# A planner that sets the order of every instruction: a finer rule for the port that VectorE and GpSimd share, lags by producing engine, four passes

## The chip, the cores and the metric

The kernel runs on one core of one Trainium2 chip. The metric is the device time of one execution in microseconds (us); three runs of the kernel before were timed. PE is TensorE, DVE VectorE, ACT ScalarE, POOL GpSimd, SP SyncE, whose queue issues most DMAs.

## The reference

Three layers follow each other on inputs of 8 batches, 8 heads, 576 positions and 64 numbers a head. Weights come as 64-bit floats.

```python
pos_block = np.arange(576) // 64
scores = np.where(pos_block[:, None] >= pos_block[None, :], q @ k.T / 8, -1e9)   # by batch and head
x = softmax(scores) @ v                              # heads side by side: 8 x 576 x 512
gate = sigmoid(sum(conv_w[j] * shift(x, 4 - j) for j in range(5)))   # causal, by channel
x = (gate * (x @ w_val)) @ w_out
xk, xr = (mu * x + (1 - mu) * shift(x, 1) for mu in (mu_k, mu_r))
out = sigmoid(xr @ w_r) * (relu(xk @ w_k) ** 2 @ w_v)               # d_ff 1024
```

## The kernel before

Every fp32 factor is split in two fp16 halves (high and low), and a product takes three matmul parts. Attention runs in 32 steps of two heads (a pair). A pair has nine score tiles (`S`, lines 748 to 763, 288 in all), which lie in turn in two halves of one PSUM tile, `sp`. For each tile: `S` on PE, `max` on DVE (line 774), `nb` (the scaled negative maximum, a 128x1 instruction on POOL or DVE, line 463), `exp` on ACT (line 777), then `rs` (row sums and reciprocal), `phi` (high half of the probabilities, `P`) and `plo` (low half, line 460 on DVE), and a DMA transpose `ptr`. Tile k+2 writes the half of `sp` that the exponential of tile k reads. `pv` (line 822) multiplies with the values into `xps`; `xhi`, `xlo`, `tap`, `conv` (line 953, reads PSUM) and `gate` make the next layers' input `xx` and the gate `tg`.

The other layers run over 13 chunks of 384 or 192 rows, all through `layer` (line 998): `V` (x @ w_val) with `gv`, `ghi`, `glo` behind it (tiles `tmp`, `gg`), `O` (w_out) with `T`, `mix`, `ymax`, `Tr`, `mixr`, `rhi`, `rlo`, then `khi`, `klo`, `Z` (w_r, the factor `wr`), `K` (w_k, tile `w3`) with `t`, `sq`, `k2h`, `k2l` (tile `kx`), and `W` (w_v, the factor `wv`) with `lo` and the store `lout`. A `W` or `Z` step is six matmuls of 512 columns. Before the first chunk the weights are loaded (`w1ld` and the like, line 554), converted in three integer steps on DVE (lines 510 to 516) and split (`h`, `o`), and `w_r`, `w_v` are read twice, first for a bound (`wrm`, `wvm`). `lodq`, `lodk`, `lodv` are the low halves of q, k and v (line 460; tiles `natqk`, `natv`); `bxr` scales `xx` anew at the end of a batch.

What order all this is issued in is not the order of the code. Each piece is an entry of `Plan` with a label (with ' for the pieces of the start), a rank, a cost on each engine that may take it, what it reads and writes, and whether it is one of those that use the port that DVE and POOL share (`share=True`). `Plan.order` walks through a modelled time: the engine that can start earliest takes the ready entry of lowest rank. `Plan.latest` walks back from the end and gives each entry its latest time, which is the rank of the next pass. The tables `OFF`, `OFF2` (added to the ranks), `PATIENCE` (how long a second engine must wait before it may take an entry) and `PREF` (the first engine) have one number per label. The framework keeps the order so found on each engine and adds the waits.

The costs and lags are numbers of the plan alone; on the chip an instruction starts as soon as its engine and its semaphores let it.

Of the kernel before, what the change touches and what calls it, by code (L numbers as in the profile page):

```python
# [32 lines left out]
class Plan:  # L33
# [5 lines left out]
    CROSS, SAME, SWITCH, DMA_OUT, DMA_IN, DMA_SET = 140, 120, 90, 1000, 650, 920  # L39
    BLOCK, WINDOW = 150, 3413  # L40
# [31 lines left out]

    def order(self, off={}, patience={}, pref={}, base=None):
# [40 lines left out]
        for _ in ops:  # L114
            while True:
                best = None
                for e, w in waiting.items():
                    if w:
                        t = max(free[e], min(w.values()))
# [10 lines left out]
            n = min((rank[x] for x, r in waiting[e].items() if r <= t))[1]  # L130
# [3 lines left out]
            if (e == POOL or (e == DVE and ops[n][7])) and ns > 130:  # L134
                t = max(t, port)
# [39 lines left out]
    def latest(self):  # L175
# [1149 lines left out]
```

## Time and profile before

| what | value |
|---|---|
| median of 3 runs | 1270.04 us (1266.98 to 1271.29) |
| the profiled execution, its own time | 1269.61 us |
| its span, first to last instruction | 1267.6 us |
| mean granted TensorE clock | 0.925 |
| busy: PE, DVE, ACT, POOL | 1027.4, 910.5, 729.3, 599.4 us |
| DMA: bytes moved, mean | 140.78 MB, 111 GB/s |

The span is 2 us shorter than the execution's time. A row of the timeline or of the waits names line, engine, operation and output<-inputs; in brackets stands how long the engine was idle before it and what ended that. A busy PE is not one at full speed: its clock is granted in two levels, and a clock of 0.9 in a stretch means that a fifth of it ran at the lower.

### The profile page before, as it was taken

How to read it: one execution, taken by the hardware profiler on the slowest of the kernel's cores; microseconds unless marked ns; L12 is line 12 of the kernel's file. 1: busy time of each engine (PE TensorE's matmuls, PEld its weight loads, DVE VectorE, ACT ScalarE, POOL GpSimd, SP SyncE). 2: the span in 40 equal slices, each digit the busy share in tenths (PEclk: the TensorE clock that was granted, in tenths of full speed). 3: DMA queues.
4: the chain of work that ended last, by engine and by line, in shares of the span. 5: the costliest groups of instructions: out<-in, count | busy, mean ns of one | idle time of the engine just before them, and what ended most of it. 6: DMA issues, size and time to landing. Idle time of an engine off the chain costs nothing. (4 is left out here: it accounts for less than half of the span.)

```text
span 1267.6 us, 20049 instructions
## 1 busy us (share of the span) xinstructions
PE 1027.4 (81%) x6695; PEld 544.5 (43%) x6695; DVE 910.5 (72%) x1984; ACT 729.3 (58%) x1583; POOL 599.4 (47%) x1185
## 2 busy tenths in 40 slices
PE   1244446699779878999899888989998799999997
PEld 0011223355434445545455454544444454444464
DVE  5787887877668787767787687677776787656441
ACT  4565566454556766656566666566666666544331
POOL 2356573322536554544646436347465546352321
PEclk9975567799899998999899889999898899999999
DMA  8597884325455774517547672366556655133000
GB/s 230 139 223 185 198 210 94 62 65 126 89 117 107 148 147 89 100 28 169 101 88 152 130 159 44 74 133 109 117 107 131 131 108 108 37 70 69 10 17 21
DMA packets 416630, 140.78 MB, mean 111 GB/s; under 512 B 402960, under 2 KB 402960, under 8 KB 416528
## 3 DMA queue, kind: packets, MB, share of 16 engines
q1 hardware_dynamic: 416032, 137.94, 51.1%
q0 software_dynamic: 496, 1.58, 0.4%
q8 instruction: 52, 0.85, 0.3%
q14 instruction: 50, 0.41, 0.1%
HBM read 49.31 MB, written 9.44 MB: 46 GB/s over the span
## 5 line engine op out<-in xcount | busy, mean ns | idle before, releaser
L463 POOL TENSOR_SCALAR smalls<-smalls 128x1 f32<-128x1 f32 (+2 forms) x607 | 212.3, 355 | 358.1 <-DVE smalls L774 213.8
L998 PEld LDWEIGHTS <-w 128*128 128x128 f16 x2640 | 246.3, 99 | 157.7 <-issue 28.3
L777 ACT ACTIVATE P<-sp,smalls 128x448 f32<-128x448 f32 (+4 forms) x288 | 183.8, 639 | 170.5 <-DVE smalls L774 45.2
L774 DVE TENSOR_REDUCE smalls<-sp 128x1 f32<-128x448 f32 (+4 forms) x288 | 145.4, 515 | 114.6 <-PE sp L763 68.4
L998 PE MATMUL fp<-wv,kx 128*128 128x512 f16 (+1 forms) x888 | 211.3, 383 | 6.7 <-DVE th L1197 5.4
L998 PE MATMUL fp<-kx,w 128*128 128x384 f16 (+1 forms) x1248 | 200.7, 314 | 2.7 <-DVE tmp L1179 2.7
L998 PEld LDWEIGHTS <-kx 128*128 128x128 f16 (+1 forms) x1332 | 124.3, 99 | 151.7 <-issue 28.2
L758 PE MATMUL sp<-qkT 128*128 128x128 f16 (+5 forms) x288 | 85.8, 313 | 100.5 <-ACT P L777 69.0
L457 POOL TENSOR_TENSOR kx<-tmp,kx 128x384 f16<-128x384 f32 (+1 forms) x144 | 132.0, 920 | 65.8 <-ACT kx L448 38.1
L998 PE MATMUL fp<-gg,w 128*128 128x385 f16 (+1 forms) x624 | 108.4, 328 | 11.2 <-DVE tmp L1100 9.0
L998 PE MATMUL fp<-wr,kx 128*128 128x512 f16 (+1 forms) x444 | 111.2, 391 | 6.2 <-DVE th L1197 4.8
L998 PE MATMUL fp<-xx,w 128*128 128x384 f16 (+1 forms) x768 | 107.6, 296 | 2.5 <-DVE tmp L1179 1.0
L953 DVE SCALAR_TENSOR_TENSOR tg<-xps,smalls,tg 128x575 f32<-128x575 f32 (+3 forms) x128 | 102.7, 803 | 0.3 <-ACT xx L448 0.2
L460 DVE SCALAR_TENSOR_TENSOR P_a<-P,smalls,P_a 128x576 f16<-128x576 f32 (+1 forms) x128 | 92.9, 733 | 3.5 <-ACT P_a L448 3.1
L758 PE MATMUL sp<-qkT,q2T 128*128 128x128 f16 (+5 forms) x288 | 91.4, 317 | 0.0
L822 PE MATMUL xps<-PT,natv 128*64 128x512 f16 (+1 forms) x720 | 76.2, 332 | 17.8 <-DMA xx<-in_moe_w_v_dram 10.9
L448 ACT ACTIVATE P_a<-P,smalls 128x576 f16<-128x576 f32 (+1 forms) x122 | 79.4, 664 | 18.2 <-DVE smalls L237 12.6
L1179 DVE TENSOR_TENSOR tmp<-fp,tmp 128x384 f32<-128x384 f32 (+1 forms) x104 | 54.3, 523 | 42.6 <-ACT tmp L1177 41.6
L1177 ACT ACTIVATE tmp<-fp 128x384 f32<-128x384 f32 (+1 forms) x104 | 48.1, 463 | 55.2 <-PE fp L998 54.8
L758 PEld LDWEIGHTS <-q2T 128*128 128x128 f16 x288 | 27.8, 101 | 113.6 <-issue 107.1
L822 PEld LDWEIGHTS <-natv 128*64 128x64 f16 x768 | 47.5, 122 | 42.5 <-issue 25.1
L450 POOL TENSOR_SCALAR kx<-tmp 128x384 f16<-128x384 f32 (+1 forms) x71 | 41.2, 584 | 48.4 <-DVE tmp L1100 35.5
(177 smaller groups left out, 1724.0 us busy)
## 6 DMA issues: line engine op xcount, KB each, us to landing
rawv<-in_v_dram SPq DMA_DIRECT2D x32, 288.0 KB, 3.4
out_dram<-th SPq DMA_DIRECT2D x35, 256.0 KB, 2.1
rawk<-in_k_dram SPq DMA_DIRECT2D x31, 288.0 KB, 3.2
rawq<-in_q_dram SPq DMA_DIRECT2D x31, 288.0 KB, 3.5
q2T<-qkT SPq DMA_DIRECT2D x60, 144.0 KB, 2.5
xx<-in_moe_w_v_dram SPq DMA_DIRECT2D x8, 512.0 KB, 4.6
tg<-in_moe_w_v_dram SPq DMA_DIRECT2D x7, 512.0 KB, 4.7
tg<-in_moe_w_k_dram SPq DMA_DIRECT2D x4, 512.0 KB, 4.6
```

The lines of the kernel that those rows point to most:

```text
L448: nc.scalar.activation(out=o, in_=i, func=AF.Copy, scale=scale)
L457: eng[e].tensor_tensor(out=o, in0=a, in1=b, op=ALU.subtract)
L460: nc.vector.scalar_tensor_tensor(out=o, in0=a, scalar=scale, in1=b, op0=ALU.mult, op1=ALU.subtract)
L463: eng[e].tensor_scalar(out=o, in0=i, scalar1=a, scalar2=b, op0=op0, op1=op1)
L758: nc.tensor.matmul(sall[:, base + c0:base + c1], qts[e][:, o + 64 * (2 * t - 1):o + 64 * (2 * t + 1)], kt[:, o + c0:o + c1], start=(e == 0 ...
L774: nc.vector.tensor_reduce(out=mx, in_=sp, op=ALU.max, axis=AX.X)
L777: nc.scalar.activation(out=P[:, 0:n], in_=sp, func=AF.Exp, scale=small["posc"][p % 3], bias=nb, accum_out=sm)
L822: nc.tensor.matmul(o, w, x, start=start, stop=stop, skip_group_check=True)
L953: lambda t=t: nc.vector.scalar_tensor_tensor(out=acc[:, t:S], in0=ps[:, 0:S - t], scalar=cx[:, 4 - t:5 - t], in1=acc[:, t:S], op0=ALU.mult ...
L998: nc.tensor.matmul(o, w, y, start=(k == i == j == 0), stop=(k == nk - 1 and i == len(ps) - 1), skip_group_check=True)
L1177: lambda fp=fp, t=t: nc.scalar.activation(out=t, in_=fp, func=AF.Relu, scale=2.0 ** -42))
L1179: lambda fp=fp, t=t: nc.vector.tensor_tensor(out=t, in0=fp, in1=t, op=ALU.mult))
```

## The change

No piece of work is added or removed. In the planner: (1) a POOL entry that is no DMA, and a DVE entry with `share`, wait in the plan until the port is free, but an engine may take another ready entry meanwhile; DVE's shared entries always hold the port, POOL's only from 300 ns on (before: any of either over 130 ns held it, and the engine stood still for it). (2) The lag between two entries goes by the engine that produces: 200, 120, 135, 70 ns for PE, DVE, ACT, POOL; before 140 across engines and 120 on one. (3) Two passes back and forth instead of one, then a last pass with the ranks of `latest`, 160 single corrections (`NUDGE`) and a third table (`OFF3`): four passes of `order`. (4) New numbers in all tables, a cost of 1040 for `pv` instead of 950, and slightly other spacings T0 and T2.

```diff
@@ -36,8 +36,10 @@
 
 
 
-    CROSS, SAME, SWITCH, DMA_OUT, DMA_IN, DMA_SET = 140, 120, 90, 1000, 650, 920
-    BLOCK, WINDOW = 150, 3413
+
+    LAG = {"PE": 200, "DVE": 120, "ACT": 135, "POOL": 70}
+    SWITCH, DMA_OUT, DMA_IN, DMA_SET = 90, 1000, 650, 920
+    BLOCK, WINDOW, SMALL = 150, 3413, 300
 
     def __init__(self):
         self.ops = []
@@ -70,6 +72,12 @@
     def transpose(self, lab, rank, blocks, reads, writes, fn, *args):
         self.add(lab, rank, self.BLOCK * blocks, [SP], reads, writes, fn, *args, dma=2)
 
+    def lag(self, d, e, f):
+
+        if e is None or f is None or e == f == PE:
+            return 0
+        return self.DMA_OUT if self.ops[d][6] else self.LAG[e]
+
     def order(self, off={}, patience={}, pref={}, base=None):
         ops = self.ops
         users = [[] for _ in ops]
@@ -81,6 +89,7 @@
         start = [0.0] * len(ops)
         taken = [None] * len(ops)
         free = {e: 0.0 for e in (PE, DVE, ACT, POOL, SP, None)}
+        turns = {DVE: [o[7] for o in ops], POOL: [not o[6] for o in ops]}
         lane = ring = port = 0.0
         live, warm, last, flying = [], False, True, []
         waiting = {e: {} for e in free}
@@ -92,10 +101,7 @@
             for f, _ in choice:
                 t = 0.0
                 for d in deps:
-                    e = taken[d]
-                    lag = 0 if e is None or (e == PE and f == PE) else (
-                        self.DMA_OUT if ops[d][6] else self.SAME if f == e else self.CROSS)
-                    t = max(t, finish[d] + lag)
+                    t = max(t, finish[d] + self.lag(d, taken[d], f))
                 waiting[f][n] = t if f == first else t + patience.get(lab, 1500.0)
 
         finish = [0.0] * len(ops)
@@ -116,7 +122,11 @@
                 best = None
                 for e, w in waiting.items():
                     if w:
-                        t = max(free[e], min(w.values()))
+                        turn = turns.get(e)
+                        if turn:
+                            t = max(free[e], min(max(r, port) if turn[x] else r for x, r in w.items()))
+                        else:
+                            t = max(free[e], min(w.values()))
                         if best is None or t < best[0]:
                             best = (t, e)
                 if not flying or (best and flying[0][0] > best[0]):
@@ -127,12 +137,12 @@
                     free[SP] = max(free[SP], lane - 950)
                 done(n)
             t, e = best
-            n = min((rank[x] for x, r in waiting[e].items() if r <= t))[1]
+            turn = turns.get(e)
+            n = min((rank[x] for x, r in waiting[e].items() if r <= t and not (turn and port > t and turn[x])))[1]
             for f, _ in ops[n][2]:
                 del waiting[f][n]
             ns = dict(ops[n][2])[e]
-            if (e == POOL or (e == DVE and ops[n][7])) and ns > 130:
-                t = max(t, port)
+            if turn and turn[n] and (e == DVE or ns >= self.SMALL):
                 port = t + ns
                 self.busy["port"] += ns
             start[n], taken[n] = t, e
@@ -188,18 +198,10 @@
         back = [0.0] * len(ops)
 
         def ready(n):
-            e = where[n]
             t = self.DMA_OUT if ops[n][6] else 0
             for u in users[n]:
-                f = where[u]
-                if e is None or f is None:
-                    lag = 0
-                elif ops[n][6]:
-                    lag = self.DMA_OUT
-                else:
-                    lag = 0 if e == f == PE else self.SAME if e == f else self.CROSS
-                t = max(t, back[u] + lag + (self.DMA_SET if ops[u][6] else 0))
-            waiting[e][n] = t
+                t = max(t, back[u] + self.lag(n, where[n], where[u]) + (self.DMA_SET if ops[u][6] else 0))
+            waiting[where[n]][n] = t
 
         for n in range(len(ops)):
             if not left[n]:
@@ -223,10 +225,17 @@
         return [end - x for x in back]
 
     def plan(self):
-        best = self.order(OFF, PATIENCE, PREF)
+        self.order(OFF, PATIENCE, PREF)
         for _ in range(ITER):
-            best = self.order(OFF2, PATIENCE, PREF, self.latest())
-        return best
+            self.order(OFF2, PATIENCE, PREF, self.latest())
+        base = self.latest()
+        seen = {}
+        for n, o in enumerate(self.ops):
+            seen.setdefault(o[0], []).append(n)
+        for lab, a, b, ns in NUDGE:
+            for n in seen[lab][a:b]:
+                base[n] += ns
+        return self.order(OFF3, PATIENCE, PREF, base)
 
     def issue(self):
         for n in self.plan():
@@ -237,105 +246,182 @@
                 fn(*args)
-ITER = 1
+ITER = 2
...
-    'K': 4.3, "K'": 7.2, "KX'": -203.8, 'O': -8.3, "O'": 36.8, 'S': -0.5, "S'": -3.9, 'T': -5.4,
+    'K': 4.3, "K'": 7.2, "KX'": -203.8, 'O': -7.0, "O'": 42.3, 'S': -0.5, "S'": -3.9, 'T': -5.4,
...
-            add("pv", e + 0.1 * part, 950, [PE], [("PT", second(p), t) for t in range(NT + 1)] + ["natvh", "natvl", ("dv", 0), ("dv", 1)],
+            add("pv", e + 0.1 * part, 1040, [PE], [("PT", second(p), t) for t in range(NT + 1)] + ["natvh", "natvl", ("dv", 0), ("dv", 1)],
...
-T0, T1, T2 = 19.8, 26.8, 71.3
+T0, T1, T2 = 20.4, 26.8, 71.2
```

Three places in the built programs show what moves. In the changed file every line behind the tables stands 86 lines lower, and 9 lines lower in the first functions.

PE, score tiles 244 and 245 of 288 (counted from 0; lines 758 and 763, both heads' factors `qkT` and `q2T`), before. The first two rows are the end of tile 244, the last two the begin of a `Z` step (`wr`):

```order
L763 LDWEIGHTS q2T_93
L763 MATMUL sp<-qkT_91,q2T_93 64x64
L758 LDWEIGHTS qkT_91
L758 MATMUL sp<-qkT_91 128x128
L758 LDWEIGHTS q2T_93
L758 MATMUL sp<-qkT_91,q2T_93 128x128
L763 LDWEIGHTS qkT_91
L763 MATMUL sp<-qkT_91 64x64
L763 LDWEIGHTS q2T_93
L763 MATMUL sp<-qkT_91,q2T_93 64x64
L998 LDWEIGHTS kx
L998 MATMUL fp_106<-wr,kx 128x512
```

The same place with the change, from the end of tile 244 on:

```order
L849 LDWEIGHTS q2T_93
L849 MATMUL sp<-qkT_91,q2T_93 64x64
L568 MATMUL sp<-ident,smalls 3x128
L1084 LDWEIGHTS kx
L1084 MATMUL fp_106<-wv,kx 128x512
```

Tile 245 stood right behind tile 244 and a `Z` step behind that; now a matmul of a scale and a whole `W` step (six such pairs, of which one is shown) stand between, and tile 245 follows these.

DVE at the same place, before; L774 is `max` of tiles 243, 244 and then 245, L460 on `natv` is `lodv`, on `P_a` `plo`, on `natqk` `lodq`:

```order
L774 TENSOR_REDUCE smalls<-sp 128x1 x2
L237 RECIPROCAL smalls<-smalls 128x2
L460 SCALAR_TENSOR_TENSOR natv<-rawv_84,smalls,natv 128x9x64
L1197 TENSOR_TENSOR th_80<-fp_106,th_80 128x512
L460 SCALAR_TENSOR_TENSOR P_a<-P_95,smalls,P_a 128x576
L774 TENSOR_REDUCE smalls<-sp 128x1
L237 RECIPROCAL smalls<-smalls 128x1
L460 SCALAR_TENSOR_TENSOR P_a<-P_96,smalls,P_a 128x576
L460 SCALAR_TENSOR_TENSOR natqk<-rawq,smalls,natqk 128x9x64
```

The same place with the change; L860 is `max` of tile 244 and then 245, L1039 `conv`, L546 `plo` (on `P_a`) and `lodq`, `lodk`:

```order
L860 TENSOR_REDUCE smalls<-sp 128x1
L549 TENSOR_SCALAR smalls<-smalls 128x3
L1039 SCALAR_TENSOR_TENSOR tg<-xps,smalls,tg 128x572
L246 RECIPROCAL smalls<-smalls 128x3
L546 SCALAR_TENSOR_TENSOR P_a<-P_95,smalls,P_a 128x576
L549 TENSOR_SCALAR smalls<-smalls 128x3
L546 SCALAR_TENSOR_TENSOR P_a<-P_96,smalls,P_a 128x576
L860 TENSOR_REDUCE smalls<-sp 128x1
L246 RECIPROCAL smalls<-smalls 128x1
L1283 TENSOR_TENSOR th_80<-fp_106,th_80 128x512
L546 SCALAR_TENSOR_TENSOR natqk<-rawq,smalls,natqk 128x9x64
L546 SCALAR_TENSOR_TENSOR natqk<-rawk,smalls,natqk 128x9x64
```

Behind the maximum of tile 244 stood a reciprocal and a split that reads two SBUF tensors (`natv`); now a tiny instruction and a `conv`, which reads PSUM, come first, and the splits of q and k stand behind the next maximum.

DVE in the start, ahead of the maxima of tiles 36 and 37 (the last row but two), before; L953 is `conv`, L510 to L516 the conversion of weights:

```order
L953 SCALAR_TENSOR_TENSOR tg<-xps,smalls,tg 128x575
L516 SCALAR_TENSOR_TENSOR xx<-xx 128x512
L953 SCALAR_TENSOR_TENSOR tg<-xps,smalls,tg 128x574
L484 TENSOR_REDUCE smalls<-sp 3x1
L953 SCALAR_TENSOR_TENSOR tg<-xps,smalls,tg 128x573
L510 TENSOR_SCALAR tg<-tg 128x512
L953 SCALAR_TENSOR_TENSOR tg<-xps,smalls,tg 128x572
L466 TENSOR_SCALAR smalls<-sp 128x3
L512 SCALAR_TENSOR_TENSOR tg<-tg 128x512
L774 TENSOR_REDUCE smalls<-sp 128x1 x2
L237 RECIPROCAL smalls<-smalls 128x3
L463 TENSOR_SCALAR smalls<-smalls 128x1
```

With the change; L543 splits `wv`, L1146 is `gv`, L546 on `gg` is `glo`, L596 to L602 the conversion:

```order
L543 TENSOR_TENSOR wv<-tg,wv 128x512
L1146 SCALAR_TENSOR_TENSOR tmp<-tg,fp_104 128x384
L546 SCALAR_TENSOR_TENSOR gg<-tmp,gg 128x384
L570 TENSOR_REDUCE smalls<-sp 3x1
L596 TENSOR_SCALAR xx<-xx 128x512
L546 SCALAR_TENSOR_TENSOR gg<-tmp,gg 128x384
L1146 SCALAR_TENSOR_TENSOR tmp<-tg,fp_105 128x384
L598 SCALAR_TENSOR_TENSOR xx<-xx 128x512
L552 TENSOR_SCALAR smalls<-sp 128x3
L602 SCALAR_TENSOR_TENSOR xx<-xx 128x512
L596 TENSOR_SCALAR tg<-tg 128x512
L860 TENSOR_REDUCE smalls<-sp 128x1 x2
```

The first chunk's `gv` and `glo` stand now ahead of these maxima, where convolution taps stood; before, the first `gv` came behind them.

Counted over the whole program: PE has 13245 instructions in both (weight loads among them), DVE 1986 and now 2053, POOL 1190 and 1120, ACT 1233 and 1245, SP 400 and 391. Twelve weight loads move from SP's queue to POOL's and three the other way. `bxr` goes from POOL to DVE in nine cases more than the other way, 29 instructions of 128x1 and 16 of 128x3 likewise.

## Rows read from the trace of the kernel before

**Rows 1.** The page: busy us (share of the span) x instructions.

```profile
PE 1027.4 (81%) x6695; PEld 544.5 (43%) x6695; DVE 910.5 (72%) x1984; ACT 729.3 (58%) x1583; POOL 599.4 (47%) x1185
```

**Rows 2.** Windows: start:end, length, busy us (x count) by engine, PEclk, DMA share, GB/s.

```profile
0.00:176.00 176.00, 62.31 (x319) 24.84 (x320) 133.20 (x294) 97.75 (x201) 86.33 (x150) 0.74 0.81 197
...
235.00:1140.00 905.00, 808.10 (x5386) 432.63 (x5386) 674.63 (x1480) 549.03 (x1205) 447.74 (x931) 0.96 0.52 106
1140.00:1268.00 128.00, 117.47 (x746) 66.41 (x744) 54.57 (x114) 44.30 (x95) 34.93 (x56) 1.00 0.11 29
977.00:981.00 4.00, 3.41 (x13) 1.24 (x12) 3.55 (x7) 3.67 (x8) 2.29 (x5) 0.60 1.16 249
```

**Rows 3.** PE's waits, 235 to 1140 us: total us, times, longest.

```profile
PE sp L758 <- ACT P L777: 27.9, 33, 2.4
PE sp L758 <- DVE smalls L774: 17.4, 19, 2.0
PE fp L998 <- DVE tmp L1100: 9.0, 4, 6.3
PE fp L998 <- DVE th L1197: 7.5, 10, 2.1
...
PE sp L482 <- DVE smalls L774: 5.2, 5, 2.8
```

**Rows 4.** Timeline of PE, 975 to 981 us.

```profile
975.11 0.22 PE L758 MATMUL sp<-qkT 128*128 128x128 f16 x1
...
976.84 0.22 PE L758 MATMUL sp<-qkT 128*128 128x128 f16 x1 [1.27 <-ACT P L777]
...
977.60 2.56 PE L998 MATMUL fp<-wr,kx 128*128 128x512 f16 x6 [0.32 <-DVE th L1197]
980.43 0.37 PE L758 MATMUL sp<-qkT 128*128 128x256 f16 x1 [0.28 <-ACT P L777]
```

**Rows 5.** Timeline of DVE in the same stretch.

```profile
975.67 0.49 DVE L774 TENSOR_REDUCE smalls<-sp 128x1 f32<-128x64 f32 x2 [0.49 <-PE sp L763]
...
976.15 0.80 DVE L460 SCALAR_TENSOR_TENSOR natv<-rawv,smalls,natv 128x576 f16<-128x576 f32 x1
...
978.88 0.82 DVE L460 SCALAR_TENSOR_TENSOR P_a<-P,smalls,P_a 128x576 f16<-128x576 f32 x1
979.61 0.81 DVE L460 SCALAR_TENSOR_TENSOR natqk<-rawq,smalls,natqk 128x576 f16<-128x576 f32 x1
```

**Rows 6.** Timeline of POOL in the same stretch.

```profile
975.07 0.19 POOL L463 TENSOR_SCALAR smalls<-smalls 128x2 f32<-128x2 f32 x1 [1.08 <-ACT P L777]
975.99 1.37 POOL L463 TENSOR_SCALAR smalls<-smalls 128x1 f32<-128x1 f32 x3 [0.73 <-DVE smalls L774]
978.90 0.85 POOL L463 TENSOR_SCALAR smalls<-smalls 128x1 f32<-128x1 f32 x1 [1.54 <-DVE smalls L237]
```

**Rows 7.** Groups by form, POOL: x count | busy us, mean ns | idle before.

```profile
L463 POOL TENSOR_SCALAR smalls<-smalls 128x1 f32<-128x1 f32 x436 | 167.7, 389 | 284.6 <-DVE smalls L774 213.8 <-DVE smalls L237 37.8 <-ACT P L777 8.5
```

**Rows 8.** Timeline of POOL and DVE, 892 to 895 us.

```profile
892.37 3.42 POOL L450 TENSOR_SCALAR xx<-xx,smalls 128x1152 f16<-128x1152 f16 x2
...
892.91 1.77 DVE L460 SCALAR_TENSOR_TENSOR natqk<-rawq,smalls,natqk 128x576 f16<-128x576 f32 x1
```

**Rows 9.** Groups by form, DVE.

```profile
L463 DVE TENSOR_SCALAR smalls<-smalls 128x1 f32<-128x1 f32 x39 | 6.2, 168 | 1.7 <-ACT th L1154 1.7
L454 DVE TENSOR_SCALAR xx<-xx,smalls 128x1152 f16<-128x1152 f16 x12 | 6.1, 518 | 0.1
...
L457 DVE TENSOR_TENSOR w<-wv,w 128x512 f16<-128x512 f32 x4 | 3.0, 762 | 0.0
```

**Rows 10.** Line 1060 (`gv`): ns min/median/max, first and last start.

```profile
L1060 DVE SCALAR_TENSOR_TENSOR tmp<-tg,fp x64: 329/446/555, 199.9 to 1214.8; 128x384 f32<-128x384 f32 x32, 128x192 f32<-128x192 f32 x32
```

**Rows 11.** Loads of w_v, last start; `W` steps, first start.

```profile
L554 SPq DMA_DIRECT2D xx<-in_moe_w_v_dram x8: 328/336/567, 97.5 to 182.7; - x8
...
L998 PE MATMUL fp<-wv,kx x888: 376/379/631, 278.9 to 1263.1; 128*128 128x512 f16 x169, 128*64 128x512 f16 x9
```

More of the change, by code (lines that the diff above doesn't have):

```diff
@@ new lines @@
+    'gc': -32.7, "gc'": 32.0, 'ghi': -41.1, "ghi'": 136.6, 'glo': -117.1, "glo'": -1.6, 'gv': -28.5,
+    "gv'": -30.3, 'hik': -53.9, "hik'": 136.8, 'hiq': 3.0, "hiq'": 41.8, 'hiv': 8.8, "hiv'": 16.2,
+    'k2h': 14.8, "k2h'": -20.0, 'k2l': -64.5, "k2l'": -37.8, 'khi': -52.0, "khi'": -147.0, 'klo': 10.3,
+    "klo'": -41.1, 'l1k': 28.6, "l1k'": 49.2, 'l1q': 76.1, "l1q'": 64.1, 'l1v': 20.5, "l1v'": 2.0,
+    'ldrawk': 88.1, "ldrawk'": -44.7, 'ldrawq': 51.7, "ldrawq'": 81.1, 'ldv': 193.1, "ldv'": 40.7,
@@ new lines @@
+    "ldrawk'": -6753, 'ldrawq': -44652, "ldrawq'": 57171, 'ldv': 80058, "ldv'": 38338, 'lo': -8490,
+    "lo'": -1, 'lodk': -47835, "lodk'": -169458, 'lodq': 6973, "lodq'": 7916, 'lodv': 2166,
+    "lodv'": 8546, 'lout': 103980, "lout'": 14357, 'lrs': 103915, "lrs'": 164274, 'lth': -21050,
+    "lth'": 73629, 'max': 709, "max'": -45797, 'mix': -69556, "mix'": -148722, 'mixr': -106835,
+    "mixr'": 114504, 'nb': -24460, "nb'": 16225, 'one': -153576, "one'": -80206, 'par': -1701,
+    "par'": -40606, 'pc': 5124, "pc'": -57042, 'phi0': 68297, "phi0'": -50938, 'phi1': -170559,
@@ L323 @@
     'T': 'ACT', "T'": 'ACT', 'Tr': 'ACT', "Tr'": 'DVE', 'bxk': 'POOL', "bxk'": 'DVE', 'bxr': 'DVE',
-    "bxr'": 'POOL', "cw'": 'DVE', 'dv': 'ACT', "dv'": 'POOL', 'gc': 'POOL', "gc'": 'DVE', 'ghi': 'ACT',
-    "ghi'": 'ACT', 'hik': 'ACT', "hik'": 'DVE', 'hiq': 'ACT', "hiq'": 'ACT', 'hiv': 'ACT', "hiv'": 'ACT',
-    'k2h': 'ACT', "k2h'": 'DVE', 'k2l': 'POOL', "k2l'": 'DVE', 'khi': 'ACT', "khi'": 'ACT', 'l1k': 'ACT',
+    "bxr'": 'POOL', 'dv': 'ACT', "dv'": 'DVE', 'gc': 'POOL', "gc'": 'POOL', 'ghi': 'ACT', "ghi'": 'ACT',
@@ L327 @@
+    'hik': 'ACT', "hik'": 'DVE', 'hiq': 'ACT', "hiq'": 'ACT', 'hiv': 'ACT', "hiv'": 'ACT', 'k2h': 'ACT',
+    "k2h'": 'DVE', 'k2l': 'POOL', "k2l'": 'DVE', 'khi': 'ACT', "khi'": 'ACT', 'l1k': 'ACT',
     "l1k'": 'ACT', 'l1q': 'ACT', "l1q'": 'ACT', 'lrs': 'POOL', "lrs'": 'POOL', 'nb': 'POOL',
-    "nb'": 'POOL', 'pc': 'DVE', "pc'": 'POOL', 'phi0': 'POOL', "phi0'": 'ACT', 'phi1': 'POOL',
-    "phi1'": 'ACT', 'phi2': 'ACT', "phi2'": 'DVE', 'phi3': 'POOL', "phi3'": 'ACT', 'phi4': 'ACT',
+    "nb'": 'POOL', 'pc': 'DVE', "pc'": 'POOL', 'phi0': 'POOL', "phi0'": 'DVE', 'phi1': 'POOL',
@@ L335 @@
-    "w3o'": 'DVE', "w3p'": 'POOL', "wr'": 'DVE', "wrh'": 'ACT', "wrld'": 'SP', "wrm'": 'DVE',
-    "wrmld'": 'SP', "wro'": 'POOL', "wv'": 'DVE', "wvh'": 'ACT', "wvld'": 'SP', "wvm'": 'DVE',
-    "wvmld'": 'SP', "wvo'": 'DVE', 'xD': 'POOL', "xD'": 'POOL', 'xhi': 'ACT', "xhi'": 'ACT',
-    'ysc': 'POOL', "ysc'": 'DVE',
+    "rlo'": 'POOL', "rs'": 'DVE', "swap0'": 'DVE', 'tap': 'ACT', "tap'": 'ACT', "w1'": 'ACT',
+    "w1h'": 'ACT', "w1ld'": 'SP', "w1o'": 'DVE', "w1p'": 'POOL', "w2h'": 'ACT', "w2ld'": 'SP',
@@ L339 @@
+    "w2o'": 'DVE', "w2p'": 'DVE', "w3h'": 'POOL', "w3ld'": 'SP', "w3o'": 'DVE', "w3p'": 'POOL',
+    "wrh'": 'ACT', "wrld'": 'SP', "wrm'": 'DVE', "wrmld'": 'SP', "wro'": 'POOL', "wv'": 'ACT',
+    "wvh'": 'ACT', "wvld'": 'POOL', "wvm'": 'DVE', "wvmld'": 'SP', "wvo'": 'DVE', 'xD': 'POOL',
+    "xD'": 'POOL', 'xhi': 'ACT', "xhi'": 'ACT', 'ysc': 'DVE', "ysc'": 'DVE',
 }
```

140 lines of the change are left out of this document (84 added, 56 removed), and 79 rows, old and new, of tables (NUDGE, OFF, OFF2, OFF3).

## The prediction

> **What bounds the kernel now.** I read the page's busy line first: TensorE (PE) is busy 1027.4 of 1267.6 us, VectorE (DVE) 72%, ScalarE (ACT) 58%, GpSimd (POOL) 47% [rows 1]. The windows then show three stages with different limits [rows 2]. Up to 176 us PE works 62 us, DVE is busy 133 us and the DMA engines 81% of the time: weights are converted and split while the first score tiles run. By 235 us the first chunk is on its way. From 235 to 1140 us PE is busy 808.1 of 905 us, so some 97 us are its idle time, at a mean granted clock of 0.96. The last 128 us are matmuls with hardly a gap. In the middle stage the list of waits says what PE waits for: score tiles of line 758 that wait for an exponential on ACT, 27.9 us in 33 waits, and for a row maximum on DVE, 17.4 us in 19 [rows 3]. That is the ring of two score halves: tile k+2 may only be written once the exponential of tile k has read its half, and that exponential stands behind `max` (DVE), then `nb` (POOL or DVE).
>
> One such place, whole [rows 4]: a score tile at 975.11 us, the next not before 976.84 (1.27 us idle), then six matmuls of a Z step, and the tile at 980.43. Behind it stand these rows of DVE and POOL [rows 5, 6]: the two maxima run at 975.67, DVE goes on with a 128x576 two-input operation at 976.15, and the three tiny POOL instructions begun at 975.99, which take 0.19 us elsewhere in the same rows, need 1.37 us together. At 978.90 another takes 0.85 us under a `plo` of 0.82 us. In this stretch the granted clock was 0.60 [rows 2], so the six Z matmuls took 2.56 us.
>
> **The port, as the trace shows it.** The three rules of the change are each seen in rows. A tiny POOL instruction waits for a DVE operation with two SBUF inputs: the 128x1 group has a mean of 389 ns [rows 7] against 0.19 us undisturbed. The reverse does not happen: the 128x576 split at 979.61 began while the POOL instruction of 978.90 was running and took 0.81 us [rows 5, 6], no more than its neighbour at 978.88. A large POOL instruction does hold DVE: two `bxr` of 3.42 us together, and under them a split of 1.77 us [rows 8]. The old rule let every POOL instruction over 130 ns hold the port, so in the plan tiny ones pushed DVE's work away, and an engine stood idle for a busy port where another ready instruction could have gone. The new one describes these rows better. If a tiny instruction held DVE all the same, the plan's new freedom would cost DVE what it saves: the last rival below.
>
> That is what the Trainium skill states ("SBUF — State Buffer", section "Who interferes with whom"): whichever starts first of a DVE instruction with two SBUF inputs and a GpSimd instruction that reads SBUF holds the shared pair for its whole length, and the other fully blocks. The row at 979.61 does not agree for an instruction of this size [rows 5, 6]; the rows of the large ones do [rows 8].
>
> **The change part by part.** No work is added or taken away: PE has the same 13245 instructions, and DVE, ACT and POOL share theirs out anew. So the sum has terms for order alone.
>
> *Spacing of the score tiles.* I counted, over the whole order, the matmuls between tile k and tile k+2, each at its undisturbed start-to-start time in the trace. From tile 54 on (about 270 us), 31 pairs before have under 2 us between them and 57 under 3 us; with the change it is 20 and 44. At the first place shown in the change's section tiles 244 and 245 stand side by side; with the change a whole W step of six matmuls comes between. 18 pairs go from close to loose, 8 the other way (the six tiles from number 101 now stand in a row, where two W steps stood among them). A wait of this kind costs (27.9 + 17.4) / (33 + 19) = 0.87 us [rows 3]. 13 fewer pairs make -11.3 us. From below: nothing, if the wait is only passed on. From above: all 18 at the 1.27 us of 976.84 [rows 4], -23 us.
>
> *`nb` behind a maximum.* On DVE 99 of 288 maxima were followed at once by an operation that takes the port while `nb` was on POOL; now it is 80 (second place: a `tg` operation that reads PSUM follows in place of the `natv` split). 19 times the mean loss of 0.389 - 0.19 = 0.20 us [rows 6, 7] is 3.8 us of chain; 52 of some 232 tiles in the stage are waited for, so 0.9 us reaches PE: -0.9, between 0 and -4.
>
> *Clock.* After such gaps PE is granted the lower of its levels, 1.2 GHz: 0.96 over 905 us [rows 2] is 0.04 x 2 x 905 = 72 us at it, which lose 36 us if PE worked throughout; some of it was idle, and I take 26. If PE's 97 us of idle time shrink by 12%, so may this: -3, between 0 and -8.
>
> *Work moved to DVE.* DVE gets 67 instructions more, POOL 70 fewer: 9 `bxr` of 0.518 us, 29 tiny ones of 0.168, about six weight differences of 0.762 [rows 9], with 16 of three columns and the smaller kinds about 18 us on an engine that is busy 75% of the middle stage. It lies in DVE's idle time unless a maximum or an `sq` stands behind it. PE's waits that DVE ended are 17.4 + 9.0 + 7.5 + 5.2 us of 905 [rows 3], 4%, with the small ones 5%; 5% to 15% of 18 us is 1 to 3: +2, between 0 and +18.
>
> *The start.* Here the order moves most. The third place shows it: ahead of tile 36's maxima DVE now has the first chunk's `gv` and `glo`, where the conversion taps stood. Summed instruction by instruction with each one's duration in this execution, DVE's work ahead of the first `gv` (199.9 us [rows 10]) falls by 11 us, ahead of the first chunk's last `klo` by 2; ahead of the second chunk's last `klo` it rises by 3. So the first chunk's two matmul layers come sooner and the gain is gone again by its third; from the second chunk on DVE is as late as before or later. Twelve weight loads move from SP's queue to POOL's, and the last of `w_v` are put 13 score tiles later (some 30 us). Now the last is issued at 182.7 us and the first W step runs at 278.9 [rows 11], 96 us later, which covers that; without this cover the first W step would be late by what is over. I take +2, between -12 (the first chunk's lead is kept) and +10.
>
> `pv`'s cost of 1040 for 950, the lags and the table entries only choose this order, and cost nothing by themselves. The last stage has the same steps behind the last score tile (16 V, 16 O, 32 W, 33 K for 35) and stays.
>
> Sum: -11.3 - 0.9 - 3 + 2 + 2 = -11.2. Against this execution's 1269.6 us, which is the median of the runs (1270.04) to 0.4, it gives **1258 us**.
>
> **The rivals.** *Start kept as well:* if the 11 us of DVE work that the first `gv` no longer waits for are kept, 1258 - 2 - 11 = 1245. For it: DVE is the busiest engine up to 176 us; against: the work is only put off to the second chunk. *No change:* the waits are passed on. Where one pair is parted another place loses its matmuls, as the six tiles in a row suggest, and PE's wait only changes its place; without the spacing and the clock it is 1269.6 - 0.9 + 2 + 2 = 1273. *Slower:* DVE becomes the limit in the middle stage. Its 18 us then lengthen the queue ahead of the maxima, no gap of PE closes, and with half of them on the path the time is 1269.6 + 9 = 1279, with all 1288. It decides when DVE's share between 235 and 1140 us passes some 85% from 75% now; 18 us in 905 is 2%, which speaks against it, and the engine's bunches (3.55 of 4 us at 977 [rows 2]) for it. *Tiny ones hold the port:* DVE's two-input operations wait for tiny POOL instructions that the plan now sets against them. Some 135 of DVE's low-half splits began under one in this execution; at 0.15 us each, most of 0.19 [rows 6], that is 20 us of DVE, and at the share above (5% to 15%) with the spacing lost 1269.6 + 4 + 2 = about 1275. The row at 979.61 speaks against it. It is the rule of the Trainium skill's page named above.
>
> **How the numbers follow.** Forecast 0.54, the start kept as well 0.13, no change 0.17, DVE the limit 0.13, tiny ones holding the port 0.03. Runs of this kernel lie 0.3% apart, so a difference under 0.3% (3.8 us) counts as none. Nearly all of the first case lies below 1266 us, and a little of the third above 1274: faster 0.66, the same 0.18, slower 0.16. The range, 1241 to 1278, reaches past the second case's 1245 and to the middle of the fourth; the forecast alone has 1249 to 1267.
>
> **What would show it.** In the profile of the changed kernel PE should be busy for over 90% of its middle stage, and the two waits of line 758 (now 844) should fall from 45.3 to some 34 us between 235 and 1140 us; the 128x1 POOL group's mean should fall below 389 ns; the clock there should be 0.96 or more; DVE's total should be near 928 us and POOL's near 560; the first `gv` should run some 10 us sooner and the second chunk at the same time as now. I would be wrong if PE's waits only change their releaser, if DVE's two-input operations grow longer than now because tiny POOL instructions hold the port after all, or if the middle stage begins later than it does now by more than the score tiles gain.

## The result, and the profile after

The changed kernel takes 1216.03 us, median of 4 runs (1214.99 to 1216.94); the kernel before 1269.44 us, median of 4. The ratio is 0.958, 95% interval 0.9561 to 0.9599. That is 53 us faster, where 11 were forecast, and it lies below the range. The profiled execution has a span of 1213.2 us, 54.4 less than before, and a mean granted clock of 0.943.

The page's busy line of the changed kernel, which answers to [rows 1]:

```profile
PE 1009.5 (83%) x6695; PEld 534.8 (44%) x6695; DVE 905.7 (75%) x2051; ACT 729.9 (60%) x1593; POOL 562.6 (46%) x1115
```

PE's idle time is the span less its busy time: 240.2 us before, 203.7 now, so 36.5 us of the 54.4. The other 18 are PE itself, which does the same matmuls in less time: at 0.925 it was granted the lower level for 0.075 x 2 x 1267.6 = 190 us, at 0.943 for 138. This split is that of the two profiled executions; what the mean clock is worth as a measure stands under the clock below.

Windows of the changed kernel, for [rows 2]. The middle stage began at 235 us and ran to 1140; its place is now 215 to 1088. The last window reaches to the second chunk's first `K` step, which stood at 307 us:

```profile
215.00:1088.00 873.00, 797.21 (x5431) 426.62 (x5430) 680.19 (x1529) 563.51 (x1237) 431.66 (x893) 0.97 0.54 110
1088.00:1214.00 126.00, 117.06 (x736) 66.05 (x734) 48.44 (x110) 41.71 (x91) 31.06 (x52) 0.99 0.11 29
0.00:286.00 286.00, 159.99 (x967) 77.61 (x968) 231.27 (x547) 165.49 (x353) 128.20 (x228) 0.83 0.69 161
```

The same window of the kernel before:

```profile
0.00:307.00 307.00, 165.06 (x969) 80.16 (x970) 235.15 (x531) 167.74 (x351) 135.80 (x242) 0.79 0.64 151
```

So the start gives 20 us (235 to 215), the middle 32 (905 to 873) and the end 2. In the start DVE's busy time hardly falls, 235.15 to 231.27, but its idle time ahead of the second chunk goes from 71.9 to 54.7 us. In the middle PE's idle time goes from 96.9 to 75.8 us (21.1) and its busy time from 808.1 to 797.2 (10.9). These two windows hold not quite the same work (5386 and 5431 matmuls). Behind the second chunk's first `K` both kernels have 5729 matmuls left:

```profile
307.00:1267.70 960.70, 862.37 (x5729) 464.31 (x5726) 675.30 (x1454) 561.57 (x1233) 463.64 (x943) 0.97 0.48 98
```

```profile
286.00:1213.30 927.30, 849.49 (x5729) 457.17 (x5727) 674.41 (x1505) 564.45 (x1241) 434.36 (x887) 0.98 0.50 102
```

This stretch is 33.4 us shorter: 20.5 of PE's idle time (98.3 to 77.8) and 12.9 of its busy time.

PE's waits of the changed kernel in its middle stage, for [rows 3]:

```profile
PE sp L844 <- DVE smalls L860: 20.4, 24, 2.6
PE sp L844 <- ACT P L863: 16.1, 23, 2.1
PE sp L574 <- ACT P L863: 6.2, 7, 1.3
PE sp L568 <- ACT P L863: 5.8, 8, 1.2
PE fp L1084 <- DVE tmp L1186: 3.4, 3, 1.9
...
PE fp L1084 <- DVE th L1283: 1.2, 2, 0.8
```

The score tiles' two waits fall from 45.3 to 36.5 us. The wait of the chunk matmuls for `mixr` (line 1186) falls from 9.0 to 3.4, that for `lo` (line 1283) from 7.5 to 1.2. These three are 8.8 + 5.6 + 6.3 = 20.7 us, about as much as the 21.1 of idle time; the smaller waits go both ways.

The line of all chunk matmuls in the changed kernel (count, ns min/median/max, first and last start):

```profile
L1084 PE MATMUL fp<-kx,w x1248: 246/326/337, 230.5 to 1197.4; 128*128 128x384 f16 x151, 128*128 128x192 f16 x28
L1084 PE MATMUL fp<-wv,kx x888: 376/379/634, 243.2 to 1208.6; 128*128 128x512 f16 x169, 128*64 128x512 f16 x9
L1084 PE MATMUL fp<-xx,w x768: 243/290/527, 153.7 to 1165.7; 128*128 128x384 f16 x96, 128*128 128x192 f16 x96
L1084 PE MATMUL fp<-gg,w x624: 246/328/528, 174.1 to 1173.7; 128*128 128x385 f16 x132, 128*128 128x193 f16 x24
```

Read with the first starts of the other kernels (same rows of each trace), these give the table on which the study of the start rests. `V` is `fp<-xx,w`, `O` `fp<-gg,w`, `K` `fp<-kx,w`, and the last column is the 97th of these, as a chunk has 96; us from the span's start:

| kernel | first `V` | first `O` | first `K` | second chunk's first `K` |
|---|---|---|---|---|
| before | 176.0 | 214.1 | 250.3 | 306.6 |
| changed | 153.7 | 174.1 | 230.5 | 286.5 |
| new start, old rest | 157.2 | 176.4 | 243.1 | 298.9 |
| new up to the second chunk, old rest | 157.2 | 176.5 | 231.2 | 287.1 |
| new order, old engines | 166.3 | 185.6 | 244.0 | 301.2 |
| changed, start on the old engines | 166.5 | 187.0 | 243.8 | 300.8 |
| changed, no single corrections | 152.1 | 174.3 | 225.8 | 288.5 |

The first `O` is 40 us sooner and half of that is gone by the first `K`, as the prediction had it in kind; but the other 20 us are still there at the second chunk, where it expected none. The first `gv` (line 1146, in answer to [rows 10]) runs 32 us sooner, not 10:

```profile
L1146 DVE SCALAR_TENSOR_TENSOR tmp<-tg,fp x64: 334/445/556, 167.5 to 1166.1; 128x384 f32<-128x384 f32 x32, 128x192 f32<-128x192 f32 x32
```

### The profile page after: what moved, and what is told of

Its sections match the earlier page's. It is cut to its first block, busy times and chain, and to the rows that moved or that the text cites. A ratio compares the mean times of both kernels' runs of the same rounds, so it can differ in the third digit from the quotient of the medians.

```text
span 1213.2 us, 20015 instructions
## 1 busy us (share of the span) xinstructions
PE 1009.5 (83%) x6695; PEld 534.8 (44%) x6695; DVE 905.7 (75%) x2051; ACT 729.9 (60%) x1593; POOL 562.6 (46%) x1115
## 5 line engine op out<-in xcount | busy, mean ns | idle before, releaser
L549 POOL TENSOR_SCALAR smalls<-smalls 128x1 f32<-128x1 f32 (+3 forms) x554 | 192.5, 351 | 358.4 <-DVE smalls L860 186.5
L1084 PEld LDWEIGHTS <-w 128*128 128x128 f16 x2640 | 242.6, 99 | 164.9 <-issue 36.2
L860 DVE TENSOR_REDUCE smalls<-sp 128x1 f32<-128x448 f32 (+4 forms) x288 | 146.7, 516 | 123.2 <-PE sp L849 57.4
L1084 PEld LDWEIGHTS <-kx 128*128 128x128 f16 (+1 forms) x1332 | 123.0, 99 | 141.2 <-issue 16.9
L543 POOL TENSOR_TENSOR kx<-tmp,kx 128x384 f16<-128x384 f32 (+1 forms) x147 | 135.0, 921 | 64.2 <-ACT kx L534 50.7
L1084 PE MATMUL fp<-xx,w 128*128 128x384 f16 (+1 forms) x768 | 107.3, 294 | 12.9 <-DVE xx L540 9.1
L1084 PE MATMUL fp<-wr,kx 128*128 128x512 f16 (+1 forms) x444 | 107.0, 383 | 2.0 <-DVE th L1283 1.2
L1039 DVE SCALAR_TENSOR_TENSOR tg<-xps,smalls,tg 128x575 f32<-128x575 f32 (+3 forms) x128 | 103.1, 805 | 5.2 <-ACT xx L534 4.1
L534 ACT ACTIVATE P_a<-P,smalls 128x320 f16<-128x320 f32 (+1 forms) x123 | 78.8, 656 | 25.1 <-issue 11.6
L546 DVE SCALAR_TENSOR_TENSOR P_a<-P,smalls,P_a 128x576 f16<-128x576 f32 (+1 forms) x128 | 88.7, 707 | 1.5 <-ACT P_a L534 1.3
L908 PE MATMUL xps<-PT,natv 128*64 128x512 f16 (+1 forms) x720 | 73.2, 323 | 0.8 <-DVE smalls L246 0.8
L849 PEld LDWEIGHTS <-qkT 128*64 128x64 f16 x256 | 28.1, 110 | 77.1 <-issue 71.5
L536 POOL TENSOR_SCALAR kx<-tmp 128x384 f16<-128x384 f32 (+1 forms) x61 | 32.1, 529 | 55.3 <-DVE tmp L1186 41.8
```

The lines of the kernel that those rows point to most:

```text
L534: nc.scalar.activation(out=o, in_=i, func=AF.Copy, scale=scale)
L543: eng[e].tensor_tensor(out=o, in0=a, in1=b, op=ALU.subtract)
L546: nc.vector.scalar_tensor_tensor(out=o, in0=a, scalar=scale, in1=b, op0=ALU.mult, op1=ALU.subtract)
L549: eng[e].tensor_scalar(out=o, in0=i, scalar1=a, scalar2=b, op0=op0, op1=op1)
L860: nc.vector.tensor_reduce(out=mx, in_=sp, op=ALU.max, axis=AX.X)
L908: nc.tensor.matmul(o, w, x, start=start, stop=stop, skip_group_check=True)
```

## The experiments

The order and the engine of every piece are two lists. Most kernels below take the changed one and replace the loop of `Plan.issue` so that either list, whole or up to a piece, is that of before. The computation is complete in each. Ratios are to the kernel before, run beside it.

**Start or rest.** Two halves, cut at the first chunk's first `K` step:

```diff
-        for n in self.plan():
+        first = [n for n, o in enumerate(self.ops) if o[0] == "K'"][0]
+        lead, rest = new, old          # the second kernel: old, new
+        part = lead[:lead.index(first)]
+        done = set(part)
+        order = part + [n for n in rest if n not in done]
+        taken = [taken_lead[n] if n in done else taken_rest[n] for n in range(len(self.ops))]
+        for n in order:
```

> The new order and engines up to the first K step of the first chunk, the old ones behind it. Start kept: the 20 us by which that step runs sooner (250 to 230 us) come from the start's own order and stay, so 1249 us (1244 to 1254). Work only put off (the prediction's step): the old rest has to do what the new start left undone, and the time is 1262 to 1272 us.

1261.99 us, ratio 0.9947 (0.9925 to 0.9969), at the edge of the branch "work only put off".

> The mirror image: the old order up to the first K step, the new one behind it. Start kept: 1216 + 20 = 1236 us (1231 to 1242), the rest's 33 us alone. Put off: 1216 to 1222 us, since the old start leaves less undone.

1240.59 us, ratio 0.9772 (0.973 to 0.9814). This is the branch "start kept", and the rest alone brings half of the 53 us. The two runs contradict each other because the seam misleads: the first kernel has the first `O` at 176.4 and loses its lead by the first `K`, at 243.1, since there the work that the new order puts off meets the old one. So the seam was moved to the second chunk's first `K` (`[16]` for `[0]`).

> As e1, with the seam at the second chunk's first K step, behind the work that the new start had put off. Start kept: the lead of 21 us at that step (307 to 286) stays whole, 1248 us (1244 to 1252), since the old rest ran at a constant lead of 7 to 9 us in e1. Put off further: the old rest gives it back as in e1, 1260 us or more.

1244.18 us, ratio 0.9819 (0.9793 to 0.9845).

> The mirror image. If start and rest add up, 1269 - 33 = 1236 us (1231 to 1241) and with e5 the two gains make the whole 53. If the rest's gain depends on the state that the new start leaves, under 25 us of gain: over 1244 us.

1248.01 us, ratio 0.9845 (0.9823 to 0.9868). Against the 1266.95 us of the kernel before, run beside both, that is -22.8 and -18.9, together 41.7 of 53; some 10 us come only with both, since the new rest gains less behind the old start. With the new start and the old rest the lead at the second chunk is 19.5 us, and it is never given back: the profiled span ends 27 us sooner (the medians differ by 22.8). The start is kept.

**Order or engines.** The old order with the new engines (`order, taken = old, taken_new`), and the reverse:

> The old order of issue, each instruction on the engine that the new plan gives it. Order is the cause: no gain, 1265 to 1290 us, since the old order was made for other engines. Engines are the cause (POOL freed of 40 us): 1235 to 1255 us.

1275.07 us, ratio 1.0062 (1.0042 to 1.0081): alone the new engines cost time.

> The new order of issue, each instruction on the engine of the kernel before. Order is the cause: 1216 to 1235 us. Order and engines only work together: 1250 us or more.

1234.67 us, ratio 0.9744 (0.9722 to 0.9766). The order alone brings 32 us, but in the start it has only 5 of the 20. Behind the second chunk's first `K` it has nearly all: 1231.5 - 301.2 = 930.3 us, for 961.0 before and 926.7 in the changed kernel. The engines are worth some 18 us, 15 of them ahead of that step, and only with the new order.

**Where in the start.** The new lists only up to the start's 27th score tile (`"S'"][27]`), some 100 us:

> The new order only up to score tile 27, which runs 26 us sooner in it (134 to 108 us). The first 100 us are the cause: a lead of 15 us or more stays to the end, 1254 us or less. The weights' work between tile 27 and the second chunk decides (put off, as the prediction had it): the lead is gone by the first K step, 1264 to 1275 us.

1268.02 us, ratio 1.0012 (0.9993 to 1.0032). The start's 41st score matmul (of those with `qkT` alone) runs at 87.5 us for 106.3 before, but the 58th, right behind the seam, at 138.1 for 134.0, and the second chunk's first `K` at 314.0: the first 100 us carry nothing by themselves. Next the 121 entries of the start that change their engine, and in another kernel the 15 loads that change their queue, go back:

```diff
-        taken = taken_new
+        taken = [taken_old[n] if o[0].endswith("'") and not o[6] else taken_new[n] for n, o in enumerate(self.ops)]
+        taken = [taken_old[n] if o[6] else taken_new[n] for n, o in enumerate(self.ops)]    # the second kernel
```

> The changed kernel with the start's 121 moved pieces that are no loads back on the engine of before; the loads stay on the new queues. The engines of the conversions are the cause: 1226 to 1236 us. SP's queue is: 1214 to 1220 us.

1226.63 us, ratio 0.9656 (0.9618 to 0.9693): 10.6 us slower than the changed kernel. The first `V` is late by 13 us, the second chunk by 14. The first 155 us of the kernel before, of the changed one and of this one, one row each in this order:

```profile
0.00:155.00 155.00, 56.67 (x275) 21.70 (x276) 112.45 (x255) 85.39 (x180) 70.14 (x131) 0.77 0.81 199
```

```profile
0.00:155.00 155.00, 56.22 (x320) 24.04 (x321) 123.61 (x292) 88.05 (x188) 69.99 (x124) 0.80 0.83 201
```

```profile
0.00:155.00 155.00, 56.77 (x315) 24.03 (x316) 112.64 (x260) 87.53 (x185) 66.66 (x125) 0.81 0.79 189
```

The fifth figure is DVE's busy time: 112.45, 123.61, and 112.64 us with the old engines. 37 of the 121 entries had gone from POOL to DVE and 21 from DVE to POOL; 25 more had gone from POOL to ACT and 21 back, 17 between DVE and ACT. With the new mix DVE has done 11 us more by 155 us. As its work up to the second chunk is no larger (231.27 us, here 232.41 up to 300 us), it is its idle time that fell. Which of these moves does it, those to DVE or those that free POOL, was not tried.

> The changed kernel with its 15 moved weight loads back on the queue of before (12 from POOL to SP, 3 from SP to POOL); order and all other engines new. In e7 the old engines cost 18 us, most of it before the second chunk. SP's queue is the cause: 1226 to 1236 us. The engines of the start's conversions are: 1214 to 1220 us.

1216.27 us, ratio 0.9579 (0.9547 to 0.961): the queue of the loads plays no part in the time.

**The spacing of the score tiles.** The changed kernel with the score tiles of 21 places drawn up again in PE's order (32 pairs with under 2 us between them; 31 before, 20 in the changed one), nothing else moved; and one in which 14 of the 20 close places are loosened further (15 left). In both, the list of the order is an edited one, and the engines are the new ones; the orders of DVE, ACT, POOL and SP stay what they are in the changed kernel:

```diff
-        for n in self.plan():
+        order, taken = EDITED, taken_new
+        for n in order:
```

> The changed kernel with PE's order altered at 21 places behind tile 54: each time the score tile is drawn up to its predecessors again, until 32 pairs have under 2 us of matmuls between them (31 before the change, 20 with it). Nothing else moves. Spacing is worth what the prediction took (0.87 us a pair, and its clock): 12 pairs more cost 10 to 15 us, 1226 to 1232 us. The spacing is worth little and the idle time was won elsewhere: 1214 to 1220 us.

1277.25 us, ratio 1.0053 (1.0026 to 1.0081): 61 us slower than the changed kernel and outside both branches. PE's waits of this kernel, 215 to 1150 us (L1461 is the score tile, L1480 the exponential, L1477 the maximum):

```profile
PE sp L1461 <- ACT P L1480: 49.7, 33, 4.7
PE sp L1461 <- DVE smalls L1477: 35.8, 32, 5.0
```

These two are 85.5 us for 36.5. A stretch of PE's timeline of it (start, us, in brackets the idle time before):

```profile
966.59 1.47 PE L1701 MATMUL fp<-wv,kx 128*128 128x512 f16 x6
967.99 0.17 PE L1191 MATMUL sp<-diag,ones 3*128 3x3 bf16 x1
971.57 0.37 PE L1461 MATMUL sp<-qkT 128*128 128x256 f16 x1 [3.40 <-DVE smalls L1477]
...
973.15 0.37 PE L1461 MATMUL sp<-qkT 128*128 128x256 f16 x1 [0.75 <-ACT P L1480]
...
973.91 5.64 PE L1701 MATMUL fp<-wv,kx 128*128 128x512 f16 x18
984.27 0.48 PE L1461 MATMUL sp<-qkT 128*128 128x384 f16 x1 [4.72 <-ACT P L1480]
```

Three tiles in a row wait 3.40, 0.75 and 4.72 us, and the 18 matmuls of three `W` steps stand in PE's queue between the second and the third, where they can fill neither large gap. Behind the first gap one of these matmuls takes 0.31 us (5.64 / 18), ahead of it 0.25 (1.47 / 6). DVE's rows tell why the third of these tiles waits so long:

```profile
971.16 0.36 DVE L1477 TENSOR_REDUCE smalls<-sp 128x1 f32<-128x192 f32 x1
...
979.58 0.69 DVE L1900 TENSOR_TENSOR th<-fp,th 128x512 f32<-128x512 f32 x1 [8.00 <-PE fp L1701]
...
981.65 0.48 DVE L1477 TENSOR_REDUCE smalls<-sp 128x1 f32<-128x320 f32 x1
```

PE had written the two tiles before it by 974. But in DVE's order `lo` of a `W` step (line 1900) stands ahead of their maxima (128x320), and that step now comes behind the tiles on PE: DVE waits 8.00 us for it, and the maxima, the exponentials and the third tile wait behind. Over the stage DVE's waits for `lo` rise from 5.4 us in the changed kernel to 12.2, those of `xkf` for ACT from 8.4 to 19.1. So the 61 us, 61 / 21 = 2.9 a place, are at least in part the price of an order on PE that no longer fits the orders of the other engines. What closeness alone costs, with all orders made to fit, no run shows.

> The changed kernel with PE's order altered the other way: at 14 of the 20 places that still have under 2 us the later tile is put behind more matmuls (15 places under 2 us are left). If each close pair costs 0.87 us: 1207 to 1212 us. If the tile that comes later only delays what hangs on it: 1214 to 1222 us.

1227.29 us, ratio 0.9665 (0.9634 to 0.9695): 11 us slower than the changed kernel and again outside both branches. The two waits are 34.0 us for 36.5, but the wait has moved to the matmul of a scale (`sp<-ident`, line 1185 here), 13.2 us for 5.8:

```profile
PE sp L1185 <- ACT P L1480: 13.2, 9, 5.4
```

More spacing is not better; with the other engines' orders left as they are, PE's order is worse off in both directions.

**Rule or numbers.** The tables, ranks and passes of before with the new rule and the lags:

> The kernel before with the new port rule and the new lags alone: old tables, two passes, no single corrections. The rule is the cause: 1235 to 1255 us, half of the gain or more. The tables and corrections are: 1262 to 1285 us, since the old tables were set for the old rule.

1311.5 us, ratio 1.0336 (1.0306 to 1.0366), slower than either branch. And the reverse, the changed kernel with the old port rule:

```diff
-        turns = {DVE: [o[7] for o in ops], POOL: [not o[6] for o in ops]}
+        turns = {}
...
-            if turn and turn[n] and (e == DVE or ns >= self.SMALL):
+            if (e == POOL or (e == DVE and ops[n][7])) and ns > 130:
+                t = max(t, port)
                 port = t + ns
```

> The changed kernel with all its tables, corrections, lags and passes, but with the old rule for the port alone (any entry of VectorE or GpSimd over 130 ns on the port holds it, and the engine stands still). Theory that the order as a whole, and not one rule, carries the 53 us: the numbers were fitted to the plan with the finer rule, so without it they point at other moments and most of the gain is gone, or the time is worse than before: 1240 to 1330 us. Rival that the numbers alone carry it: within 8 us of the changed kernel's 1216 us. The old numbers with the new rule took 1311.5 us.

1304.98 us, ratio 1.03 (1.0245 to 1.0356). Neither half alone is any good. The new lags are in both kernels; they were not tried alone. Last, the changed kernel with the loop over `NUDGE` left empty:

```diff
-        for lab, a, b, ns in NUDGE:
+        for lab, a, b, ns in []:
```

> The changed kernel without the 160 single corrections (the plan's last pass is still made, with the third table). Theory that the rule, the lags and the tables by label already give an order that suits the chip and the corrections only polish it: 1216 to 1232 us, at least 35 of the 53 us kept. Rival that the order is a fit in which the single corrections carry as much as the rule: 1240 us or more.

1245.34 us, ratio 0.9829 (0.9779 to 0.9878), 22.7 us below the 1268.06 of the kernel before, run beside it. This is the rival's branch. The kernel has nearly the whole start (the table: 288.5 us for 286.5), so the 160 corrections carry most of the middle. Its middle stage and PE's waits there:

```profile
218.00:1116.00 898.00, 809.38 (x5422) 429.63 (x5420) 676.73 (x1551) 557.75 (x1230) 424.68 (x884) 0.96 0.53 107
```

```profile
PE sp L844 <- ACT P L863: 26.7, 25, 2.8
PE sp L844 <- DVE smalls L860: 12.0, 15, 2.5
PE fp L1084 <- DVE th L1283: 6.6, 5, 3.0
PE fp L1084 <- DVE tmp L1186: 5.7, 4, 2.7
```

It has 18 pairs of score tiles under 2 us, fewer than the changed kernel's 20, and yet 38.7 us of waits for 36.5, and a middle stage of 898 us for 873. The kernel with the old port rule has 21 such pairs and these rows between 250 and 1180 us:

```profile
PE sp L845 <- ACT P L864: 32.0, 29, 3.2
PE sp L845 <- DVE smalls L861: 19.8, 21, 2.4
```

51.8 us, more than the kernel before with its 31 pairs. The number of close pairs does not foretell the wait.

## Why the prediction was wrong

The direction held, and so did what was to be seen in the middle stage: PE is busy 91% of it (797.2 of 873 us), the clock is 0.97, the two waits fell. But one term had the wrong sign (the start), one was far too small (the clock), and one was not in the sum (the waits of the chunk matmuls).

**The step that failed first is "The start".** It stands at +2 us and measured -20. It summed DVE's busy time ahead of each milestone, found 3 us more ahead of the second chunk's, and concluded that "from the second chunk on DVE is as late as before or later". That takes DVE's idle time as given. DVE's work up to that `K` was about the same (235.15 and 231.27 us, where 3 us more were forecast), but DVE stood idle 71.9 us there and now 54.7. Nothing is paid back: with the old rest behind the new start the lead stays to the end. The rival "start kept as well" had the right outcome, at 11 us for 20. What shortens the idle time is order and engines together: the order alone gives 5 us at the second chunk, the old order with the new engines loses time. Of the 17.2 us less, 12.6 lie ahead of the start's 27th score tile (37.5 us idle up to 134 us, now 24.9 up to 108; one row before, one of the changed kernel):

```profile
0.00:134.00 134.00, 48.66 (x235) 18.29 (x235) 96.47 (x217) 74.05 (x155) 62.20 (x114) 0.80 0.80 198
```

```profile
0.00:108.00 108.00, 41.22 (x228) 17.20 (x229) 83.11 (x200) 65.15 (x140) 46.25 (x87) 0.90 0.84 200
```

In the kernel before, the list of DVE's waits up to there begins with

```profile
DVE smalls L774 <- PE sp L763: 10.5, 9, 1.9
DVE xx L510 <- DMA xx<-in_moe_w_val_dram: 7.9, 1, 7.9
```

and in the changed kernel, up to the same tile at 108 us, these two read

```profile
DVE xx L596 <- DMA xx<-in_moe_w_val_dram: 3.3, 1, 3.3
...
DVE smalls L860 <- PE sp L849: 2.7, 6, 0.8
```

Both were in the trace of before, and the prediction did not look at what DVE waits for. But shorter waits there are not enough: the kernel that has the new lists only up to that tile has them too (3.2 and 2.7 us up to 109), and by its second chunk DVE has stood idle 81.0 us:

```profile
0.00:314.00 314.00, 164.02 (x964) 80.30 (x965) 233.03 (x537) 166.54 (x351) 134.01 (x236) 0.78 0.62 148
```

The lead is kept only where the work up to the second chunk is in the new order too.

**The clock** was sized at 3 us and measured 12.9 behind the second chunk's first `K`, where the matmuls left are the same (862.4 to 849.5 us), and 18 over the span. The time at the lower level was worked out rightly (0.04 x 2 x 905 = 72 us), but its reduction was taken as 12%. The 0.97 of now is too coarse for it (44 to 61 us); as the span's 138 less 0.21 x 2 x 215 = 90 of the start (0.79 up to 215 us) and some 2 of the end, it is about 45 us by estimate, more than a third less. PE's idle time fell by 22%, not 12%. That the busy time goes with the clock is seen across kernels: a matmul of the middle stage is 146.8 ns of busy time on the mean in the changed kernel and 147.3 with looser tiles (both 0.97), 150.0 before, 149.5 with the tiles drawn up and 149.3 without single corrections (all 0.96), 150.3 with the old port rule (0.95).

The mean clock of a whole execution is a poor measure of this. In 45 further executions of the kernel before it lies between 0.922 and 0.969, in 30 of them over 0.94, as high as in the changed kernel; their median time is 1267.8 us and that of the other 15 1269.7. No trace of one of the 30 was kept.

**The waits of the chunk matmuls** for `mixr` and `lo`, 9.0 and 7.5 us in [rows 3], were not in the sum as a gain (they stand only in the 4% by which the moved work is weighed); the prediction read the order of the score tiles alone. They gave 11.9 us. Without the single corrections the one for `lo` is still 6.6 us, so these corrections take it away; which of them do was not tried.

**The spacing** was forecast at -11.3 us and the two waits fell by 8.8. The 13 pairs are those under 3 us (57 to 44); of those under 2 us there are 11 fewer, which at 0.87 us make 9.6. That the size is right owes much to chance all the same: two kernels with about 20 close pairs have 38.7 and 51.8 us of waits, and the one before, with 31, has 45.3. A count of pairs times a mean wait leaves out where they stand, what is queued behind, and what the other engines' orders want first.

**`nb` behind a maximum** was not confirmed. The POOL group of [rows 7] in the changed kernel:

```profile
L549 POOL TENSOR_SCALAR smalls<-smalls 128x1 f32<-128x1 f32 x407 | 156.5, 388 | 268.7 <-DVE smalls L860 186.5 <-DVE smalls L246 36.7 <-DVE smalls L549 16.1
```

388 ns for 389: a tiny instruction still waits for the port as long. **Work moved to DVE** cost nothing to be seen: DVE's total fell to 905.7 us where 928 was forecast, POOL's 562.6 is as forecast. With the order alone DVE's busy time for the same 1984 instructions is 16.9 us less (910.5 to 893.6 in the run with the old engines), and the new engines add 12.1, not 18. One kind that became shorter, the splits of the probabilities, before and after:

```profile
L460 DVE SCALAR_TENSOR_TENSOR P_a<-P,smalls,P_a 128x576 f16<-128x576 f32 x64 | 54.4, 861 | 1.8 <-ACT P_a L448 1.8
```

```profile
L546 DVE SCALAR_TENSOR_TENSOR P_a<-P,smalls,P_a 128x576 f16<-128x576 f32 x64 | 52.6, 834 | 0.6 <-ACT P_a L534 0.6
```

**Tiny ones hold the port**, the last rival, is settled by the same traces. The low-half splits of 128x576 (of `P_a`, `natqk` and `natv`) that met no POOL instruction but tiny ones (those that write `smalls`) took 810 ns on the mean where a tiny one was running as they began (34 of them, at most 822) and 810 where none was (67); in the changed kernel it is 808 (30) and 808 (78). Those that met a larger POOL instruction took 1014 ns (57), now 965 (50), and there lies most of the change of the mean from 861 to 834. The Trainium skill ("SBUF — State Buffer", section "Who interferes with whom") calls the port pair an exclusive lock, for which a DVE instruction with two SBUF inputs contends with a GpSimd instruction that reads SBUF, and has the order of issue decide who blocks, not the shape. The larger ones agree; that a tiny one holds DVE up is not borne out here.

"No change" and "DVE the limit" fell with the result; DVE's share in the middle rose to 78% only.

**Still open.** Some 10 us come only when start and rest are both new, and no run singles out the pieces that bring them. Nor was it tried which of the 160 corrections matter, or what the lags, the cost of `pv`, the spacings and the third table do alone. That DVE's idle time ahead of the second chunk fell with the start's gain, and that it needs the new engines, is shown by the windows and by the swap of engines; which of the entries opens which gap, and whether a gap of DVE or of POOL had to close, is not.

## What to carry to other kernels

When an order changes, do not sum only an engine's work ahead of a milestone: where it stands idle for a good part of the stretch (here DVE for 71.9 of 307 us), its idle time can be the larger lever, so list what it waits for there and ask of each wait whether the new order fills it. Price a wait in a queue that issues in order by what stands ready behind it and by what the other engines' orders want first, not by the mean of the waits now listed; and look for PE's clock to move with its idle time. A planner's rule and the numbers fitted to it are one thing: each without the other made this kernel 3% slower.

## What the runs showed of the hardware

Three things were not expected. The 21 score tiles drawn up on PE alone cost 61 us, of which PE's idle time between 215 us and the end of the middle stage is 43.8 us ((935 - 815.4) less (873 - 797.2)) and its longer busy time, at a granted clock of 0.96 for 0.97, 18.2, as much as the whole change gained. Fifteen weight loads, fourteen of them of 512 KB, moved from one issuing queue to another changed nothing in the time (1216.27 for 1216.03 us). And a 128x576 split on DVE that begins while a tiny POOL instruction runs takes 810 ns as it does without one, while those that met a larger POOL instruction took 1014.
